# Infini-attention with a GeGLU FFN on one core: two phases, transposed scores, four heads per PE tile set, softmax without maximum behind a guard

## Chip, cores, metric

One core of one Trainium2 chip. The metric is the device time of one execution in microseconds (us), median over several runs; lower is better.

## The reference, cut to what matters

x is 2048 x 448 (bf16), 16 heads of 28, four segments of 512 rows, FFN width 1792. Inside a segment the attention is causal; between segments a linear memory is read and then updated.

```python
xn = layernorm(x)
for s in range(4):                                   # segments of 512 rows
    logits = qs @ ks.T * 28**-0.5 + causal_mask
    a_dot = softmax(logits) @ vs
    pq = phi(qs)                                     # phi(t) = t+1 if t>0 else exp(t)
    a_mem = (pq @ M) / (pq @ z + 1e-6)
    o = g * a_mem + (1 - g) * a_dot                  # g = sigmoid(beta), one per head
    M, z = M + phi(ks).T @ vs, z + phi(ks).sum()
s = concat(o) @ wo
g = silu((gelu(xn @ w_gate) * (xn @ w_up)) @ w_down)
out = x + s * g
```

## The kernel before

Segment by segment: load x, layer norm, projection, attention, memory update, FFN, store. In attention, one step takes one block of 128 queries and two heads. Scores have queries on partitions; DVE masks, takes the maximum and negates it; ACT takes the exponential; the result is transposed on PE, copied back from PSUM by DVE and ACT, and multiplied with V, 29 columns at a time (28 and a column of ones, which yields the denominator).

```python
        def stage_scores(j, hp):
            w = (j + 1) * P
            s_ps = ps_big.tile([P, 2, 512], F32, name="big")
            for i in range(2):
                g, hh = divmod(2 * hp + i, HG)
                nc.tensor.matmul(out=s_ps[:, i, 0:w],
                                 lhsT=qT[hh * HP:(hh + 1) * HP, g, j * P:(j + 1) * P],
                                 rhs=kT[hh * HP:(hh + 1) * HP, g, 0:w], start=True, stop=True)
            nc.vector.tensor_tensor(out=s_ps[:, :, j * P:w], ..., in1=cmask..., op=ALU.add)   # cut
            nc.vector.reduce_max(out=mx[:], in_=s_ps[:, :, 0:w], axis=AX.X)
            nc.vector.tensor_scalar(out=nb_[:], in0=mx[:], scalar1=-scale, scalar2=None, op0=ALU.mult)
            for i in range(2):
                nc.scalar.activation(out=p_sb[:, i, 0:w], in_=s_ps[:, i, 0:w], func=ACT.Exp,
                                     bias=nb_[:, i:i + 1], scale=scale)
            return p_sb

        def stage_pv(j, hp, p_sb, o_v3):
            for i in range(2):
                h = 2 * hp + i
                for kb in range(j + 1):
                    nc.tensor.transpose(pt_ps[:, kb, :], p_sb[:, i, kb * P:(kb + 1) * P], ident[:])
                # cut: copy pt_ps to pt_sb, on DVE for i == 0, on ACT for i == 1
                for kb in range(j + 1):
                    nc.tensor.matmul(out=o_v3[:, h, 0:Dh + 1], lhsT=pt_sb[:, kb, :],
                                     rhs=va[:, kb, h, 0:Dh + 1], start=(kb == 0), stop=(kb == j))
        # cut: per query block, reciprocal of the denominators, memory read, mix, transposes, output projection
        # cut: memory update, then the FFN of the same segment
```

Of the kernel before, what the change touches and what calls it, by code (L numbers as in the profile page):

```python
# [8 lines left out]
ACT = mybir.ActivationFunctionType  # L9
ALU = mybir.AluOpType  # L10
F32 = mybir.dt.float32
BF16 = mybir.dt.bfloat16
AX = mybir.AxisListType


@with_exitstack
def kernel(
    ctx: ExitStack,
    tc: tile.TileContext,
    A_x: bass.AP,  # L20
# [9 lines left out]
    out: bass.AP,  # L30
):
    nc = tc.nc
    P = 128
    x2 = A_x.flatten_outer_dims()
    o2 = out.flatten_outer_dims()
    S, D = x2.shape
    F = B_w_gate.shape[1]
    H = A_beta.shape[0]
    Dh = D // H
    NSEG = 4  # L40
    L = S // NSEG
    NB = L // P
    HP = 32
    HG = 3
    G = (H + HG - 1) // HG
    GP = HG * HP

    def gsz(g):
        return min(HG, H - g * HG)
    DC = 112  # L50
    NDC = D // DC
    NFC = F // P
    scale = float(Dh) ** -0.5
    EPS = 1e-5
    assert D == NDC * DC and H * Dh == D and F == NFC * P and L == NB * P
    assert Dh < HP and NB * P <= 512 and H * HP <= 512

    const = ctx.enter_context(tc.tile_pool(name="const", bufs=1))
    wld = ctx.enter_context(tc.tile_pool(name="wld", bufs=1))
    segp = ctx.enter_context(tc.tile_pool(name="segp", bufs=2))  # L60
    work = ctx.enter_context(tc.tile_pool(name="work", bufs=2))
    seg1 = ctx.enter_context(tc.tile_pool(name="seg1", bufs=1))
    attn = ctx.enter_context(tc.tile_pool(name="attn", bufs=3))
    small = ctx.enter_context(tc.tile_pool(name="small", bufs=4))
# [4 lines left out]
    ident = const.tile([P, P], BF16, name="ident")  # L69
# [2 lines left out]
    make_causal_mask(nc, cmask[:], mask_val=-1e9)  # L72
    bdmask = const.tile([GP, GP], F32, name="bdmask")
    nc.vector.memset(bdmask[:], 0.0)
    for i in range(HG):
        nc.vector.memset(bdmask[i * HP:(i + 1) * HP, i * HP:(i + 1) * HP], 1.0)

    beta_bf = const.tile([P, H], A_beta.dtype, name="beta_bf")
# [5 lines left out]
                            op0=ALU.mult, op1=ALU.add)  # L84
# [11 lines left out]
    wo_sb = const.tile([DC, NDC, D], A_wo.dtype, name="wo_sb")  # L96
    wg_sb = const.tile([DC, NDC, F], B_w_gate.dtype, name="wg_sb")
    wu_sb = const.tile([DC, NDC, F], B_w_up.dtype, name="wu_sb")
    wd_sb = const.tile([P, NFC, D], B_w_down.dtype, name="wd_sb")

    def late_weight_loads():
# [10 lines left out]
                          in_=wq_raw[:].rearrange("p c (h d) -> p c h d", d=Dh))  # L112
    nc.gpsimd.tensor_copy(out=wkp[:, :, :, 0:Dh],
                          in_=wk_raw[:].rearrange("p c (h d) -> p c h d", d=Dh))

    vaug = []
    pkb = []
    for i in range(2):
        v_t = const.tile([P, NB, H, HP], BF16, name=f"vaug{i}")
# [3 lines left out]
        k_t = const.tile([P, NB, H, HP], BF16, name=f"pkb{i}")  # L123
        nc.gpsimd.memset(k_t[:], 0.0)
        pkb.append(k_t)
    macc = const.tile([GP, G, GP], F32, name="macc")
    mbd = const.tile([GP, G, GP], BF16, name="mbd")

# [7 lines left out]
    x_v = x2.rearrange("(s b p) d -> s p b d", p=P, b=NB)  # L136
    o_v = o2.rearrange("(s b p) d -> s p b d", p=P, b=NB)

    for s in range(NSEG):
        use_mem = s > 0  # L140
        upd_mem = s < NSEG - 1
        va = vaug[s % 2]
        pk = pkb[s % 2]
# [7 lines left out]
        for b in range(NB):  # L151
# [5 lines left out]
                                op0=ALU.add)  # L157
# [14 lines left out]
        for g in range(G):  # L172
            n = gsz(g) * HP
            for (wp, dst, is_q) in ((wqp, qT, True), (wkp, kT, False)):
                pr = ps_acc.tile([P, L], F32, name="acc")
                for c in range(NDC):
                    nc.tensor.matmul(  # L177
                        out=pr[:n, :],
                        lhsT=wp[:, c, g * HG:g * HG + gsz(g), :].rearrange("p h d -> p (h d)"),
                        rhs=xnT[:, c, :], start=(c == 0), stop=(c == NDC - 1))  # L180
                nc.scalar.copy(out=dst[:n, g, :], in_=pr[:n, :])  # L181
                if is_q and use_mem:
                    phi(pqT[:n, g, :], pr[:n, :], [P, L], n)
# [22 lines left out]
        def stage_scores(j, hp):  # L206
            w = (j + 1) * P
            s_ps = ps_big.tile([P, 2, 512], F32, name="big")
            for i in range(2):
                g, hh = divmod(2 * hp + i, HG)  # L210
                nc.tensor.matmul(out=s_ps[:, i, 0:w],  # L211
                                 lhsT=qT[hh * HP:(hh + 1) * HP, g, j * P:(j + 1) * P],
                                 rhs=kT[hh * HP:(hh + 1) * HP, g, 0:w],
                                 start=True, stop=True)
            nc.vector.tensor_tensor(out=s_ps[:, :, j * P:w], in0=s_ps[:, :, j * P:w],  # L215
                                    in1=cmask[:].unsqueeze(1).to_broadcast([P, 2, P]),
                                    op=ALU.add)
            mx = small.tile([P, 2], F32, name="mx")
            nc.vector.reduce_max(out=mx[:], in_=s_ps[:, :, 0:w], axis=AX.X)  # L219
            nb_ = small.tile([P, 2], F32, name="nb_")  # L220
            nc.vector.tensor_scalar(out=nb_[:], in0=mx[:], scalar1=-scale, scalar2=None,
                                    op0=ALU.mult)
            p_sb = attn.tile([P, 2, L], BF16, name="p_sb")
# [4 lines that stand above are left out]
# [77 lines left out]
        if upd_mem:  # L305
            for g in range(G):
                n = gsz(g) * HP
                hs = slice(g * HG, g * HG + gsz(g))
                u_ps = ps_acc.tile([P, L], F32, name="acc")
                for b in range(NB):  # L310
                    nc.tensor.matmul(
                        out=u_ps[:n, 0:n],
                        lhsT=pk[:, b, hs, :].rearrange("p h d -> p (h d)"),
                        rhs=va[:, b, hs, :].rearrange("p h d -> p (h d)"),
                        start=(b == 0), stop=(b == NB - 1))
                if s == 0:
                    nc.vector.tensor_tensor(out=macc[:n, g, 0:n], in0=u_ps[:n, 0:n],
                                            in1=bdmask[:n, 0:n], op=ALU.mult)
                else:
                    um = work.tile([GP, GP], F32, name="um")  # L320
                    nc.vector.tensor_tensor(out=um[:n, 0:n], in0=u_ps[:n, 0:n],
                                            in1=bdmask[:n, 0:n], op=ALU.mult)
                    nc.gpsimd.tensor_tensor(out=macc[:n, g, 0:n], in0=macc[:n, g, 0:n],
                                            in1=um[:n, 0:n], op=ALU.add)
                nc.gpsimd.tensor_copy(out=mbd[:n, g, 0:n], in_=macc[:n, g, 0:n])
# [22 lines left out]
        nc.sync.dma_start(out=o_v[s], in_=o_out[:])  # L348


# [1 line left out]
_INS = ['A_x', 'A_wq', 'A_wk', 'A_wv', 'A_wo', 'A_beta', 'B_x', 'B_w_gate', 'B_w_up', 'B_w_down']  # L352
_OUTS = [((1, 2048, 448), 'bfloat16')]
# [25 lines left out]
```

## Time and profile before

| | before |
|---|---|
| median of 4 runs | 570.84 us (566.3 to 573.75) |
| span of the profiled run, mean granted clock of PE | 566.7 us, 0.762 |
| start, until attention | 42 us |
| four attention stages | 296 us |
| three projection stages between segments | 72 us |
| four FFN stages | 150 us |
| end | 7 us |

The prediction below shows the lines and reads them.

### The profile page before, as it was taken

What the parts mean: (1) busy time and instruction counts of PE and PEld (TensorE: products, weight loads), DVE (VectorE), ACT (ScalarE), POOL (GpSimd) and SP (SyncE); (2) the same over time, 40 slices, a digit from 0 to 9 for tenths busy, and PEclk for the clock granted to TensorE, in tenths of its full rate; (3) what the DMA queues carried; (4) which work ended last, traced back from release to release, by engine and by line L of the source; (5) the groups of instructions that cost most, each with busy time, mean ns of one, the idle gap of its engine ahead of it and who ended that gap; (6) DMA issues with size and microseconds to landing.
All of it is one profiled execution on the core that took longest, in us unless ns stands there. A gap on an engine that the chain in (4) does not pass through costs nothing.

```text
span 566.7 us, 7756 instructions
## 1 busy us (share of the span) xinstructions
PE 446.8 (79%) x2864; PEld 226.6 (40%) x2864; DVE 333.0 (59%) x826; ACT 301.6 (53%) x605; POOL 70.2 (12%) x91
## 2 busy tenths in 40 slices
PE   0776877899976679688997677768999867968895
PEld 0432444444532334344453233434445433434342
DVE  7338787643057787765308778784422678776430
ACT  1465666544357566563447655656335656656441
POOL 9000000010600000003060000000214000000006
PEclk9995565599977555579999655576999955557998
DMA  7910000000010000000010000000000000000000
GB/s 189 275 56 1 1 0 2 1 0 2 33 33 0 2 0 2 2 0 2 1 38 29 1 1 0 2 2 0 1 1 32 1 1 2 0 2 1 0 1 33
DMA packets 6422, 10.59 MB, mean 19 GB/s; under 512 B 384, under 2 KB 5392, under 8 KB 6384
## 3 DMA queue, kind: packets, MB, share of 16 engines
q0 software_dynamic: 1088, 5.62, 3.6%
q1 hardware_dynamic: 4368, 3.67, 2.2%
q10 hardware_dynamic: 928, 0.80, 0.5%
q8 instruction: 22, 0.36, 0.3%
q14 instruction: 16, 0.13, 0.1%
HBM read 8.26 MB, written 1.84 MB: 18 GB/s over the span
## 4 chain that ended last, share of the span: by engine, by line
PE 59%; DVE 16%; ACT 13%; DMA 4%; issue 4%; POOL 3%; SPq 0%; POOLq 0%; ACTq 0%; DVEq 0%
PE big L332 17%; PE tp L234 10%; PE acc L342 7%; PE acc L177 7%; ACT p_sb L225 6%; DVE mx L219 5%; PE big L211 5%; PE acc L286 4%; DVE big L215 4%; DMA x_sb<-in_A_x_dram 4%; ACT pt_sb L240 3%; PE big L189 2%; POOL o_sb L272 2%; PE acc L242 2%; DVE pt_sb L238 2%
## 5 line engine op out<-in xcount | busy, mean ns | idle before, releaser
L234 PE MATMUL tp<-ident,p_sb 128*128 128x128 bf16 x640 | 100.2, 283 | 19.0 <-ACT p_sb L225 16.4
L219 DVE TENSOR_REDUCE mx<-big 128x2 f32<-128x256 f32 (+3 forms) x128 | 104.4, 816 | 1.6
L240 ACT COPY pt_sb<-tp 128x128 bf16<-128x128 bf16 (+3 forms) x128 | 54.5, 426 | 57.6 <-PE tp L234 52.8
L211 PE MATMUL big<-kT,qT 32*128 32x128 bf16 (+3 forms) x256 | 61.3, 420 | 15.3 <-ACT p_sb L225 12.7
L215 DVE TENSOR_TENSOR big<-big,cmask 128x256 f32<-128x256 f32 x128 | 55.0, 430 | 27.4 <-PE big L211 14.3
L234 PEld LDWEIGHTS <-p_sb 128*128 128x128 bf16 x640 | 53.4, 119 | 42.1 <-ACT p_sb L225 37.3
L242 PE MATMUL acc<-vaug,pt_sb 128*128 128x29 bf16 x640 | 56.0, 192 | 16.8 <-DVE pt_sb L238 7.4
L336 DVE TENSOR_TENSOR hT<-gl,big 128x512 bf16<-128x512 bf16 x56 | 38.4, 686 | 51.2 <-ACT gl L335 51.2
L335 ACT ACTIVATE gl<-big 128x512 bf16<-128x512 f32 x56 | 33.0, 597 | 57.4 <-PE big L332 57.3
L242 PEld LDWEIGHTS <-pt_sb 128*128 128x128 bf16 x640 | 38.3, 108 | 62.8 <-DVE pt_sb L238 17.9
L332 PE MATMUL big<-xnT,wg_sb 112*128 112x512 bf16 x224 | 62.9, 397 | 0.5 <-DVE hT L336 0.5
L332 PE MATMUL big<-xnT,wu_sb 112*128 112x512 bf16 x224 | 61.5, 387 | 0.0
L238 DVE COPY pt_sb<-tp 128x128 bf16<-128x128 bf16 (+3 forms) x128 | 40.8, 319 | 31.6 <-PE tp L234 28.9
L342 PE MATMUL acc<-wd_sb,hT 128*128 128x448 bf16 x224 | 43.0, 352 | 0.0
L177 PE MATMUL acc<-xnT,wqp 112*96 112x512 bf16 (+1 forms) x96 | 27.2, 409 | 7.9 <-ACT kT L181 7.9
L177 PE MATMUL acc<-xnT,wkp 112*96 112x512 bf16 (+1 forms) x96 | 28.5, 425 | 6.0 <-DVE pqT L133 6.0
L332 PEld LDWEIGHTS <-wg_sb 112*128 112x128 bf16 x224 | 22.2, 101 | 23.8 <-issue 2.0
L189 PE MATMUL big<-wkv,xnT 112*128 112x448 bf16 x128 | 30.2, 362 | 1.9 <-DVE pkb L199 1.7
L211 PEld LDWEIGHTS <-qT 32*128 32x128 bf16 x256 | 16.1, 98 | 37.7 <-issue 30.5
L281 PE MATMUL tp<-ident,o_sb 128*112 128x128 bf16 x64 | 9.8, 301 | 26.8 <-POOL o_sb L272 23.3
L332 PEld LDWEIGHTS <-wu_sb 112*128 112x128 bf16 x224 | 21.7, 99 | 22.8
L342 PEld LDWEIGHTS <-hT 128*128 128x128 bf16 x224 | 21.9, 98 | 20.7
(355 smaller groups left out, 539.7 us busy)
## 6 DMA issues: line engine op xcount, KB each, us to landing
x_sb<-in_A_x_dram SPq DMA_DIRECT2D x4, 448.0 KB, 6.6
out_dram<-o_out SPq DMA_DIRECT2D x4, 448.0 KB, 2.9
wg_sb<-in_B_w_gate_dram POOLq DMA_DIRECT2D x1, 1568.0 KB, 10.2
wu_sb<-in_B_w_up_dram POOLq DMA_DIRECT2D x1, 1568.0 KB, 16.3
wd_sb<-in_B_w_down_dram POOLq DMA_DIRECT2D x1, 1568.0 KB, 19.9
wk_raw<-in_A_wk_dram ACTq DMA_DIRECT2D x1, 392.0 KB, 5.4
wo_sb<-in_A_wo_dram ACTq DMA_DIRECT2D x1, 392.0 KB, 11.3
wq_raw<-in_A_wq_dram POOLq DMA_DIRECT2D x1, 392.0 KB, 9.0
```

The lines of the kernel that those rows point to most:

```text
L177: nc.tensor.matmul(out=pr[:n, :], lhsT=wp[:, c, g * HG:g * HG + gsz(g), :].rearrange("p h d -> p (h d)"), rhs=xnT[:, c, :], start=(c == 0) ...
L189: nc.tensor.matmul(out=kv[:, i, 0:D], lhsT=xnT[:, c, b * P:(b + 1) * P], rhs=wkv[:, c, i * D:(i + 1) * D], start=(c == 0), stop=(c == NDC ...
L211: nc.tensor.matmul(out=s_ps[:, i, 0:w], lhsT=qT[hh * HP:(hh + 1) * HP, g, j * P:(j + 1) * P], rhs=kT[hh * HP:(hh + 1) * HP, g, 0:w], start ...
L215: nc.vector.tensor_tensor(out=s_ps[:, :, j * P:w], in0=s_ps[:, :, j * P:w], in1=cmask[:].unsqueeze(1).to_broadcast([P, 2, P]), op=ALU.add)
L219: nc.vector.reduce_max(out=mx[:], in_=s_ps[:, :, 0:w], axis=AX.X)
L234: nc.tensor.transpose(pt_ps[:, kb, :], p_sb[:, i, kb * P:(kb + 1) * P], ident[:])
L238: nc.vector.tensor_copy(out=pt_sb[:, 0:j + 1, :], in_=pt_ps[:, 0:j + 1, :])
L240: nc.scalar.copy(out=pt_sb[:, 0:j + 1, :], in_=pt_ps[:, 0:j + 1, :])
L242: nc.tensor.matmul(out=o_v3[:, h, 0:Dh + 1], lhsT=pt_sb[:, kb, :], rhs=va[:, kb, h, 0:Dh + 1], start=(kb == 0), stop=(kb == j))
L332: nc.tensor.matmul(out=gu[:, i, :], lhsT=w_sb[:, c, fc * P:(fc + 1) * P], rhs=xnT[:, c, :], start=(c == 0), stop=(c == NDC - 1))
L336: nc.vector.tensor_tensor(out=hT[:, fc, :], in0=gl[:], in1=gu[:, 1, :], op=ALU.mult)
L342: nc.tensor.matmul(out=d_ps[:, 0:D], lhsT=hT[:, fc, b * P:(b + 1) * P], rhs=wd_sb[:, fc, :], start=(fc == 0), stop=(fc == NFC - 1))
```

## The change

The intent: shorten the chain around the exponential. (1) Scores are made transposed, keys on partitions, so the exponential's output is already the operand of the product with V: no transposes and no copies. (2) Four heads share the PE array: scores use row strips of 32, V products use four column strips. (3) The softmax takes no maximum; a guard on the norms of wq and wk bounds the logits, and if it fails, the old kernel runs as a fallback. (4) The causal triangle is set to zero on POOL after the exponential. (5) Denominators go through DRAM, to be inverted compactly and loaded back broadcast over the rows of a head. (6) All attention first, then all FFN, so the output projection of attention is taken in the FFN phase.

```diff
+        BANKS = (((0, 0),), ((1, 0), (3, 384)), ((2, 0),))
+        def scores(s, g, bk):
+            w = sum(L - kb * P for kb, _ in BANKS[bk])
+            for pr in range(2):
+                sp = ps_s.tile([P, 2, L], F32, name="s")
+                for kb, c0 in BANKS[bk]:
+                    n = L - kb * P
+                    for j in range(2):
+                        r = slice((2 * pr + j) * HP, (2 * pr + j + 1) * HP)
+                        nc.tensor.matmul(out=sp[:, j, c0:c0 + n],
+                                         lhsT=kT[s][r, g, kb * P:(kb + 1) * P],
+                                         rhs=qT[s][r, g, kb * P:L], start=True, stop=True)
+                pt = ptp.tile([P, 2, L], BF16, name="pt")
+                nc.scalar.activation(out=pt[:, :, 0:w], in_=sp[:, :, 0:w], func=ACT.Exp, scale=scale)
+                for kb, c0 in BANKS[bk]:
+                    v = pt[:, :, c0:c0 + P]
+                    nc.gpsimd.affine_select(out=v, in_=v, pattern=[[0, 2], [1, P]],
+                                            compare_op=ALU.is_ge, fill=0.0, base=0, channel_multiplier=-1)
+        def pv(s, g, bk, pts, acc):    # cut: n = L - kb * P, va = V and ones of segment s
+            for kb, c0 in BANKS[bk]:
+                for i in range(HG):
+                    nc.tensor.matmul(out=acc[i * HP:(i + 1) * HP, kb * P:L],
+                                     lhsT=va[:, kb, g * HG + i, :], rhs=pts[i // 2][:, i % 2, c0:c0 + n],
+                                     start=(kb == 0), stop=(kb == 2), tile_position=(0, i * HP))
+        def evac(s, g, side, ps):          # side 0: attention, side 1: memory; cut: t, a result tile oU of a pool of 5 per side
+            nc.vector.tensor_copy(out=t[:], in_=ps[:])
+            nc.sync.dma_start(out=den[s][side, g * HG:(g + 1) * HG, :], in_=t[Dh:P:HP, :])
+        def normalise(s):
+            # ... cut: load den as 128 x 64, add 1e-6, times 1/gate, reciprocal, store to rdr
+            for g in range(G):
+                for side in range(ns):
+                    r = rbp.tile([P, L], F32, name=f"rb{side}")
+                    nc.sync.dma_start(out=r[:],
+                        in_=rdr[side, g * HG:(g + 1) * HG, :].unsqueeze(1).to_broadcast([HG, HP, L]))
+                    rb.append(r)
+                # cut: rb = the group's tiles, o_a and o_n its results, the case s == 0 without memory
+                nc.gpsimd.tensor_tensor(out=o_a[:], in0=o_a[:], in1=rb[0][:], op=ALU.mult)
+                nc.gpsimd.tensor_tensor(out=o_n[:], in0=o_n[:], in1=rb[1][:], op=ALU.mult)
+                nc.gpsimd.tensor_tensor(out=dst, in0=o_a[:], in1=o_n[:], op=ALU.add)
...
+        for s in range(NSEG):              # phase 1
+            # ... cut: load x(s+1); per group and bank: scores, the pending V product, evac, memory read;
+            # ... cut: normalise(s) once its last group is out; layer norm and projection of s+1; update(s)
+        ok = nc.values_load(oki[0:1, 0:1], min_val=0, max_val=1)
+        tc.no_sync_barrier()
+        for s in range(NSEG):              # phase 2: FFN as before, plus oT @ wo
...
+    ok = fast_path(tc, ...)
+    with tc.If(ok == 0, preferred_fallthrough_block=False):
+        general_path(tc, ...)              # the kernel before
```

## The prediction

> **What bounds the kernel now.** I read the page's busy shares and its slices first, to see whether one engine is full.
>
> ```profile
> span 566.7 us, 7756 instructions
> PE 446.8 (79%) x2864; PEld 226.6 (40%) x2864; DVE 333.0 (59%) x826; ACT 301.6 (53%) x605; POOL 70.2 (12%) x91
> ...
> PEclk9995565599977555579999655576999955557998
> ```
>
> No engine is full, and the granted clock changes between about 5 and 10 tenths four times: there are stages of two kinds, once per segment. So I cut the span by stage (columns: busy us of PE, weight load, DVE, ACT, POOL, then the granted clock).
>
> ```profile
> 0.00:42.00 42.00, 21.12 (x98) 11.29 (x99) 20.03 (x46) 17.44 (x29) 13.76 (x17) 1.00 0.65 175
> 42.00:113.00 71.00, 54.01 (x404) 28.03 (x403) 53.54 (x142) 43.56 (x99) 0.00 (x0) 0.54 0.00 1
> 113.00:151.00 38.00, 37.38 (x219) 18.65 (x217) 12.86 (x26) 14.52 (x24) 7.91 (x12) 1.00 0.00 1
> 151.00:176.00 25.00, 18.65 (x78) 9.13 (x76) 13.63 (x31) 16.54 (x29) 2.16 (x2) 0.86 0.13 37
> 176.00:253.00 77.00, 58.03 (x433) 29.76 (x433) 58.56 (x158) 46.13 (x104) 3.38 (x3) 0.56 0.00 1
> 560.00:567.00 7.00, 0.00 (x0) 0.00 (x0) 0.00 (x0) 0.31 (x1) 2.16 (x2) 0.72 0.19 66
> ```
>
> The pattern repeats. The four attention stages (42 to 113, 176 to 253, 315 to 395, 453 to 521) last 296 us, the four FFN stages 150, the three projection stages between segments 72, the start 42, the end 7. An FFN stage is PE-bound at full clock: 37.4 of 38 us. An attention stage has PE and DVE both at about 75% and the clock at 0.54 to 0.60: a chain of short hand-offs at a slow clock. The chain of waits and the cost groups say which ones.
>
> ```profile
> PE big L332 17%; PE tp L234 10%; PE acc L342 7%; PE acc L177 7%; ACT p_sb L225 6%; DVE mx L219 5%; PE big L211 5%; PE acc L286 4%; DVE big L215 4%; DMA x_sb<-in_A_x_dram 4%; ACT pt_sb L240 3%; PE big L189 2%; POOL o_sb L272 2%; PE acc L242 2%; DVE pt_sb L238 2%
> ...
> L234 PE MATMUL tp<-ident,p_sb 128*128 128x128 bf16 x640 | 100.2, 283 | 19.0 <-ACT p_sb L225 16.4
> L219 DVE TENSOR_REDUCE mx<-big 128x2 f32<-128x256 f32 (+3 forms) x128 | 104.4, 816 | 1.6
> L240 ACT COPY pt_sb<-tp 128x128 bf16<-128x128 bf16 (+3 forms) x128 | 54.5, 426 | 57.6 <-PE tp L234 52.8
> L215 DVE TENSOR_TENSOR big<-big,cmask 128x256 f32<-128x256 f32 x128 | 55.0, 430 | 27.4 <-PE big L211 14.3
> L242 PE MATMUL acc<-vaug,pt_sb 128*128 128x29 bf16 x640 | 56.0, 192 | 16.8 <-DVE pt_sb L238 7.4
> L238 DVE COPY pt_sb<-tp 128x128 bf16<-128x128 bf16 (+3 forms) x128 | 40.8, 319 | 31.6 <-PE tp L234 28.9
> ```
>
> Around the exponentials there is masking (55.0), maximum (104.4), 640 transposes (100.2), copies of them (54.5 on ACT, 40.8 on DVE) and 640 products only 29 columns wide (56.0). All of this goes or shrinks. Last, the timeline, for the durations I need.
>
> ```profile
> 510.13 0.39 PE L211 MATMUL big<-kT,qT 32*128 32x512 bf16 x1
> 510.88 0.39 PE L211 MATMUL big<-kT,qT 32*128 32x512 bf16 x2
> 513.05 1.27 ACT L225 ACTIVATE p_sb<-big,nb__5581 128x512 bf16<-128x512 f32 x2 [0.58 <-DVE nb__5581 L221]
> ...
> L346 POOL TENSOR_TENSOR sl<-sl,sA 128x448 f32<-128x448 f32 x16 | 18.1, 1131 | 94.6 <-ACT sl L345 94.6
> masks.py:199 POOL TENSOR_SCALAR_AFFINE_SELECT ident<-ident 128x128 bf16<-128x128 bf16 x1 | 0.3, 296 | 0.0
> ```
>
> One score matmul of 512 columns takes 0.39 us, and two of them, in different row strips, also take 0.39 us together, at the full clock of that stretch. One streams for 0.217 (90 FFN matmuls of 512 columns take 19.53 us in the chain), so two in series would take about 0.6: they ran side by side.
>
> **What the Trainium skill says.** "TensorEngine Tiling (Array Packing)", Key Properties: different tiles execute loads and matmuls in parallel, and changing the tiling mode drains the engine. The pair above agrees with the first; no trace here shows the second. Its Performance Considerations add that tiling "speeds up TensorE but not PSUM evacuation", which is why I expect ACT, not PE, as the floor of the softmax itself. "TensorE: Matmul & The Clock Gate", Part 1: the clock is half when the array has not been busy, full after some 3.4 us of sustained work; the trace agrees (0.54 to 0.60 in attention, 1.00 in FFN). "GPSIMD Engine Reference", section 3.1: two-input elementwise work costs about 2.6 cycles per element; the trace's 1131 ns for 448 is 2.5 ns each, rather worse. "DMA: Bandwidth & Descriptors", Anatomy of one DMA: about 2 us fixed; the 448 KB stores of this trace land in 2.9.
>
> **The change, part by part.** All attention now comes first, then all FFN. Scores are made transposed (keys on partitions), so the exponential's output feeds the product with V directly.
>
> *ACT.* Per segment and group of four heads, exponentials of 1024, 1024, 1024, 1024, 512 and 512 columns. The timeline's two of 512 in 1.27 us, each 0.69 long, put the second 0.58 after the first; 384 columns take 0.578 and 512 take 0.690, so 1024 is about 0.58 + 0.45 = 1.03. Sum: 16 x (4 x 1.03 + 2 x 0.58) = 84.5 us, against 120 busy for the same lines before. With 24 exponentials for phi at 0.55 to 0.60: 98 us in the attention phase.
>
> *DVE.* Mask, maximum, negation and copies go (220 us). It takes over the PSUM copies: 32 of Q and K and 28 of results at about 0.69, 16 of V at 0.6, phi 24, layer norm 26, the rest 5: about 106 us.
>
> *POOL.* 128 triangle selects of 256 elements, about 0.40 each (0.296 for 128, plus 128 at memset's 0.84 ns): 51. Normalisation, 40 tensor_tensors of 512 at 1.29 (1131 ns scaled): 52. Updates 6: about 109 us, where before it had 14 in the attention stages.
>
> *PE, at full clock.* Scores come in pairs, since two heads share a PSUM tile and the other two wait for the second: 2 x 1280 columns per group, 1.07 us, x16 = 17. The product with V has four column strips together: 1280 columns, 0.53 us, x16 = 8.5. Projection: 128 of 512 at 0.217 and 112 of 448 at 0.19 = 49 (six groups of three heads become four of four, so 64 fewer). Transposes 6.5, updates 3.4, memory reads 2.6. Sum 87 us; at the attention clock of 0.56 it is 155.
>
> *DMA.* The denominators go to DRAM and back: store, load, reciprocal, store, broadcast loads, four round trips of about 2 us per segment. It frees DVE of per-row work, but DVE and POOL are in-order, so a late landing holds the triangle selects behind it.
>
> *FFN.* The same 448 matmuls at 0.217 (97.2), 224 at 0.1895 (42.4: 56 took 10.61) and 64 output projections (12.1): 152 us, already at full clock before. No gain.
>
> **Attention phase in sum.** ACT 98, DVE 106, POOL 109, PE 87 to 155: four engines balanced, so none hides behind another. Projections and layer norm of the next segment have PSUM of their own and depend only on x; instructions are not issued strictly in program order (in the trace FFN matmuls begin at 109.5 while attention products run at 113), so I let them overlap attention. With POOL at the 75% that the old attention reached on its busiest engines: 109 / 0.75 = 145; with PE at a clock of 0.65, 87 / 0.65 = 134 plus drains and waits of some 20. Four segments at about 36 plus three normalisation hand-offs at about 4: I choose 158 us. The start falls to about 36 (x lands at 13 as now, layer norm 8, projection 13 to 15). Entering FFN: 5 for the last round trip, which stands before FFN's multiplies on DVE. End 7, branch over the fallback path 4 (my guess). Sum: 36 + 158 + 5 + 152 + 11 = 362; measured time is 4 over the span now, so **366 us**, 36% less.
>
> **The rivals.**
> 1. *POOL and DMA serialise the segments.* If normalisation stands in POOL's queue ahead of the next segment's selects, each segment boundary costs some 9 us of round trips plus 12 multiplies and adds (15), less about 5 of work ahead: 20 x 3, giving about 415. For: strict order within an engine, POOL at 1131 ns for 448. Against: the order seen is chosen by readiness.
> 2. *PE at half clock is the bound.* 87 us become 174 with drains on top: attention 190, total about 400. For: clock 0.50 in most attention windows although PE is marked 75% busy. Against: a PE that becomes the bound is dense and gets its clock back, as the old projections did (0.86 to 1.00).
> 3. *Everything overlaps.* Attention 115 to 120, total about 325. For: balanced engines, separate PSUM. Against: the old attention with two stages in flight never passed 77%.
> 4. *The guard and fallback cost more than a branch.* Waiting for the guard value or skipping 7000 instructions: +5 to +20. Nothing in this trace shows it.
>
> **Range and chances.** Rivals 1 and 2 span 400 to 415, rival 3 gives 325; together they make 328 to 415. For no gain at all attention would have to cost 350 us, more than before; only a mistake in kind would do that. Faster by over 2%: 0.98; within 2%: 0.01; slower: 0.01.
>
> **What would show it.** Right: a first phase of about 195 us with exponentials on ACT near 85 us, POOL over 100 us busy, and a second phase of about 155 to 160 us at clock 1.00 with PE full. Score pairs of 512 columns in one streaming time, V products four to a streaming time. Rival 1: POOL idle for DMA with selects late, ACT idle about 20 us at each boundary. Rival 2: attention windows at 0.50 with PE full. Wrong outright: matmuls in column strips running in series (PE 25 us longer at full clock), selects of far over 0.4 us, or an FFN clock below 1.

## The result and the profile after

376.92 us median of 4 runs (376.23 to 378.08), against 570.84. The ratio is 0.6609, with a 95% interval of 0.6572 to 0.6646. A ratio here is the mean time of one kernel's fast runs over that of the other's fast runs of the same rounds, so not quite the ratio of the medians. The output is correct; the fallback was not taken.

The page of the changed kernel, its span, busy times and granted clock:

```profile
span 375.8 us, 4396 instructions
PE 308.9 (82%) x1619; PEld 128.8 (34%) x1620; DVE 159.6 (42%) x297; ACT 146.4 (39%) x203; POOL 142.0 (38%) x207
PEclk9999999995559965559855589999999999999998
```

DVE and ACT have half the work that they had (333.0 and 301.6 us), POOL twice (70.2). The clock row splits in two: from the middle on full clock, in the first part three dips to half. Cut by stage (columns: busy us of PE, weight load, DVE, ACT, POOL, then clock, DMA share, GB/s):

```profile
0.00:37.30 37.30, 15.25 (x52) 6.06 (x53) 23.02 (x51) 1.58 (x3) 16.38 (x15) 1.00 0.79 209
37.30:214.70 177.40, 140.02 (x834) 50.25 (x833) 86.65 (x173) 93.64 (x121) 94.02 (x164) 0.74 0.10 36
214.70:368.40 153.70, 153.66 (x736) 72.48 (x736) 49.27 (x74) 51.14 (x80) 30.61 (x27) 0.99 0.12 36
```

The attention phase, with the projections of three segments inside it, takes 177.4 us, where attention and projections took 296 + 72 = 368. That is 190.6 of the 190.9 us by which the span fell; the start gave about 5 and the FFN took back about 4. The costliest groups of the new attention phase (in each line: busy us, mean ns of one, then the idle time of the engine before them and what ended most of it):

```profile
L252 ACT ACTIVATE pt<-s 128x1024 bf16<-128x1024 f32 (+1 forms) x96 | 81.8, 881 | 93.4 <-PE s L248 66.7
L255 POOL TENSOR_SCALAR_AFFINE_SELECT pt<-pt 128x256 bf16<-128x256 bf16 x128 | 52.9, 432 | 64.2 <-ACT pt L252 63.4
L266 PE MATMUL pv<-pt,vaug 128*32 128x128 bf16 (+3 forms) x256 | 37.7, 378 | 21.6 <-POOL pt L255 21.1
L248 PE MATMUL s<-qT,kT 32*128 32x128 bf16 (+3 forms) x256 | 43.0, 361 | 7.2 <-POOL mbd L234 5.0
L312 POOL TENSOR_TENSOR oU<-oU,rb 128x512 f32<-128x512 f32 x12 | 15.2, 1266 | 20.9 <-DVE hT L362 12.4
```

The exponentials (81.8) stand alone where maximum, mask, transposes and copies stood around them. But ACT waits 66.7 us for scores, and PE waits 21.1 us for the selects that POOL makes. Where those waits lie is seen in stretches of 10 us:

```profile
100.00:110.00 10.00, 10.00 (x50) 2.40 (x51) 2.79 (x7) 6.14 (x8) 3.32 (x8) 0.50 0.00 1
130.00:140.00 10.00, 2.59 (x25) 1.04 (x22) 1.13 (x2) 4.38 (x6) 7.74 (x9) 0.69 0.26 102
140.00:150.00 10.00, 5.13 (x27) 1.86 (x26) 3.94 (x6) 2.05 (x2) 8.29 (x9) 0.50 0.25 91
```

At the boundary of two segments (130 to 150) PE works 7.7 of 20 us, POOL 16.0, and the DMA share stands at a quarter. Between boundaries (100 to 110) PE is marked busy all the time, but at half clock. The timeline of the boundary, with lines on strips first and last (start, duration; in brackets the idle time before and what ended it):

```profile
130.49 0.40 PE L266 MATMUL pv<-pt,vaug 128*32 128x512 bf16 x4
136.70 1.26 POOL L233 TENSOR_TENSOR macc<-macc,um 128x512 f32<-128x512 f32 x1
139.12 0.61 POOL L234 CAST mbd<-macc 128x512 bf16<-128x512 f32 x1
139.79 1.03 PE L282 MATMUL m<-pqT,mbd 128*128 128x512 bf16 x2 [4.92 <-POOL mbd L234]
145.15 1.02 ACT L252 ACTIVATE pt<-s 128x1024 bf16<-128x1024 f32 x1 [9.11 <-PE pv L266]
...
207.12 0.60 PE L248 MATMUL s<-qT,kT 32*128 32x512 bf16 x1
208.74 0.61 PE L248 MATMUL s<-qT,kT 32*128 32x512 bf16 x2
```

PE waits 4.92 us for the memory's bf16 copy, which stands in POOL's queue between normalisation multiplies, and at 145.15 ACT has been idle for 9.11 us, until V products let it go on. The last two lines, both at half clock: one score matmul of 512 columns takes 0.60 us, two in different row strips take 0.61. They run side by side. So do column strips: in the first line, at full clock, four V products of 512 columns take 0.40 us, and in series they would take 0.87 (an estimate: four times the 0.217 of the prediction's FFN matmuls).

Why is the DMA share a quarter? The broadcast loads have a slowest dimension of 4 (the heads of a group). The Trainium skill, "DMA: Bandwidth & Descriptors", section "Why a DMA increments its semaphore by 16 and not by 1", says that a load uses the largest number of engines up to 16 that divides the slowest dimension of both sides: 4. The trace agrees: share 0.26 at 102 GB/s, so one load of 256 KB takes about 2.6 us, and eight of them about 21 us at a boundary (an estimate; the first boundary has four loads, as segment 0 reads no memory).

### The profile page after: what moved, and what is told of

Its sections match the earlier page's. It is cut to its first block, busy times and chain, and to the rows that moved or that the text cites. A ratio compares the mean times of both kernels' runs of the same rounds, so it can differ in the third digit from the quotient of the medians.

```text
span 375.8 us, 4396 instructions
## 1 busy us (share of the span) xinstructions
PE 308.9 (82%) x1619; PEld 128.8 (34%) x1620; DVE 159.6 (42%) x297; ACT 146.4 (39%) x203; POOL 142.0 (38%) x207
## 5 line engine op out<-in xcount | busy, mean ns | idle before, releaser
L252 ACT ACTIVATE pt<-s 128x1024 bf16<-128x1024 f32 (+1 forms) x96 | 81.8, 881 | 93.4 <-PE s L248 66.7
L255 POOL TENSOR_SCALAR_AFFINE_SELECT pt<-pt 128x256 bf16<-128x256 bf16 x128 | 52.9, 432 | 64.2 <-ACT pt L252 63.4
L362 DVE TENSOR_TENSOR hT<-gl,s 128x512 bf16<-128x512 bf16 x56 | 38.2, 687 | 63.5 <-ACT gl L361 63.5
L358 PE MATMUL s<-xnT,wg_sb 112*128 112x512 bf16 x224 | 58.8, 386 | 0.1
L358 PE MATMUL s<-xnT,wu_sb 112*128 112x512 bf16 x224 | 58.4, 384 | 0.0
L361 ACT ACTIVATE gl<-s 128x512 bf16<-128x512 f32 x56 | 33.1, 597 | 63.5 <-PE s L358 63.5
L266 PE MATMUL pv<-pt,vaug 128*32 128x128 bf16 (+3 forms) x256 | 37.7, 378 | 21.6 <-POOL pt L255 21.1
L248 PE MATMUL s<-qT,kT 32*128 32x128 bf16 (+3 forms) x256 | 43.0, 361 | 7.2 <-POOL mbd L234 5.0
L367 PE MATMUL pv<-wd_sb,hT 128*128 128x448 bf16 x224 | 44.3, 352 | 0.0
L182 PE MATMUL m<-xnT,wq_pad 112*128 112x512 bf16 x64 | 22.3, 468 | 6.9 <-DVE qT L186 5.5
L312 POOL TENSOR_TENSOR oU<-oU,rb 128x512 f32<-128x512 f32 x12 | 15.2, 1266 | 20.9 <-DVE hT L362 12.4
L374 ACT ACTIVATE sl<-pv 128x448 f32<-128x448 f32 x16 | 8.7, 544 | 26.8 <-PE pv L367 26.8
```

The costliest lines, as they stand in the source:

```text
L182: nc.tensor.matmul(out=pr[:], lhsT=wpad[nm][:, c, g * HG:(g + 1) * HG, :].rearrange("p h d -> p (h d)"), rhs=xnT[:, c, s, :], start=(c == ...
L248: nc.tensor.matmul(out=sp[:, j, c0:c0 + n], lhsT=kT[s][r, g, kb * P:(kb + 1) * P], rhs=qT[s][r, g, kb * P:L], start=True, stop=True)
L252: nc.scalar.activation(out=pt[:, :, 0:w], in_=sp[:, :, 0:w], func=ACT.Exp, scale=scale)
L255: nc.gpsimd.affine_select(out=v, in_=v, pattern=[[0, 2], [1, P]], compare_op=ALU.is_ge, fill=0.0, base=0, channel_multiplier=-1)
L266: nc.tensor.matmul(out=acc[i * HP:(i + 1) * HP, kb * P:L], lhsT=va[:, kb, g * HG + i, :], rhs=pts[i // 2][:, i % 2, c0:c0 + n], start=(kb ...
L312: nc.gpsimd.tensor_tensor(out=o_a[:], in0=o_a[:], in1=rb[0][:], op=ALU.mult)
```

## The experiments

Two things hold for all of them. First, the build arranges each engine's stream anew for each kernel, so an edit also moves the order of instructions that it does not touch; where that matters, it is said. Second, each was timed in three rounds beside the kernel before (571 us); all profiled runs were fast unless said.

**1. The normalisation's 40 multiplies and adds on DVE instead of POOL**

```diff
-  nc.gpsimd.tensor_tensor(out=o_a[:], in0=o_a[:], in1=rb[0][:], op=ALU.mult)   # and the three like it
+  nc.vector.tensor_tensor(out=o_a[:], in0=o_a[:], in1=rb[0][:], op=ALU.mult)
```

> The changed kernel with the normalisation's 40 multiplies and adds moved from POOL to DVE; nothing else. Theory 1 (POOL's queue: the attention phase, 178 us against the 158 predicted, loses its time at segment boundaries because triangle selects stand behind normalisation arithmetic in one in-order queue): the ACT gaps of 9 us at 136 to 145 us and after 190 us shrink, total 352 to 364 us. Theory 2 (the DRAM round trip: what holds the queue is the landing of the broadcast loads, whoever waits): the same wait moves to DVE, which also copies projections and results out of PSUM, total 370 to 385 us.

Measured: 398.31 us, ratio 0.6995 (0.6953 to 0.7036); 21 us slower than the changed kernel, and outside the ranges of both theories. Attention does end earlier, with the last V product at 204.8 and not 214.2. But the timeline at the entry to the FFN shows the loss:

```profile
217.32 0.69 DVE L312 TENSOR_TENSOR oU<-oU,rb 128x512 f32<-128x512 f32 x1 [6.82 <-DMA rb<-rdr]
219.99 0.69 DVE L313 TENSOR_TENSOR oU<-oU,rb 128x512 f32<-128x512 f32 x1 [1.98 <-DMA rb<-rdr]
...
238.90 1.86 PE L358 MATMUL s<-xnT,wg_sb 112*128 112x512 bf16 x4 [26.56 <-DVE hT L362]
```

DVE waits for each load of the last segment, one every 2.6 us or so, and the FFN's own multiply stands behind them in DVE's queue: PE is idle for 26.56 us. So in this build the loads are slow, and a slow load costs what stands behind it in the same queue. On POOL, the last segment's normalisation lies beside the FFN, and PE does not wait there.

**2. x of the second segment loaded before the FFN weights**

```diff
+        load_x(1)
         nc.sync.dma_start(out=wg_sb[:], ...)
...
-            if s + 1 < NSEG:
+            if 1 < s + 1 < NSEG:
```

> The changed kernel with the load of the second x segment issued ahead of the three FFN weight loads. In the trace DVE stands idle 7.2 us at 22 to 29 us before the layer norm statistics of segment 1, whose x lands behind 4.7 MB of weights, and PE waits 5.5 us for DVE's copy behind it. If that is the start's loss: total 5 to 7 us less, 370 to 372 us. Rival: the start is bound by the POOL squares and layer norm in any case or the time is given back at the first boundary: total within 2 us of 377.

Measured: 378.09 us, ratio 0.6632 (0.6592 to 0.6673); no gain. The first exponential starts at 28.4 and not 37.3, yet the last V product starts at 215.2 against 214.2. The nine microseconds are all given back in the phase, as the rival had it. What takes them back was not looked for.

**3. Normalisation with a constant in place of the loads (wrong)**

```diff
-                    r = rbp.tile([P, L], F32, name=f"rb{side}")
-                    nc.sync.dma_start(out=r[:], in_=rdr[side, ...].to_broadcast([HG, HP, L]))
-                    rb.append(r)
+                rb = [rb_c] * ns            # one tile of ones
```

> Wrong results on purpose: the normalisation multiplies by a constant tile, so its arithmetic stays on POOL but nothing waits for the 28 broadcast loads, which are gone. Theory 1 (POOL's arithmetic in the queue): the boundaries stay, only the 20 us of POOL waits for those loads go and part of them is hidden; total 364 to 374 us. Theory 2 (the round trip holds the queue): the boundary gaps close, total 340 to 358 us.

Measured: 365.11 us median, two runs fast (359.95 and 362.39), two slow; the ratio of the fast runs is 0.6338 (0.6285 to 0.6392), which is 4.1% less than the changed kernel's 0.6609, some 15 us. That lies between the two expected ranges, so neither theory alone. The edit takes away all waiting for the denominators (store, inversion, loads), not the loads only, and keeps the multiplies: about 15 us, from two runs, is the price of the whole round trip. The profiled run was one of the slow ones.

**4. The memory update's add and copy on DVE instead of POOL**

```diff
-                nc.gpsimd.tensor_tensor(out=macc[:], in0=macc[:], in1=um[:], op=ALU.add)
-            nc.gpsimd.tensor_copy(out=mbd[:], in_=macc[:])
+                nc.vector.tensor_tensor(out=macc[:], in0=macc[:], in1=um[:], op=ALU.add)
+            nc.vector.tensor_copy(out=mbd[:], in_=macc[:])
```

> The changed kernel with only the memory update's add and bf16 copy (5 instructions) moved from POOL to DVE. PE waits for that copy 4.9 + 10.7 us in the trace, with scores and V products queued behind. If the copy's place in POOL's queue is what opens the 9 us gap at the boundary: total 8 to 14 us less, 363 to 369 us. If the selects behind normalisation would hold PE there anyway: within 3 us of 377.

Measured: 374.59 us, ratio 0.6589 (0.6543 to 0.6635): 2 us, within the intervals of both. The rival came true; more was expected. The wait for that copy was real (4.92 us), but PE's wait for selects grew: by the groups, V products wait 31.7 us for POOL's selects, where it was 21.1. The selects stand in the same queue as the multiplies. Taking one victim out of a queue leaves the others in it; that this is why the gain did not come is argued.

**5. Each broadcast load split by head**

```diff
-                    nc.sync.dma_start(out=r[:],
-                        in_=rdr[side, g * HG:(g + 1) * HG, :].unsqueeze(1).to_broadcast([HG, HP, L]))
+                    for i in range(HG):
+                        nc.sync.dma_start(out=r[i * HP:(i + 1) * HP, :],
+                            in_=rdr[side, g * HG + i:g * HG + i + 1, :].to_broadcast([HP, L]))
```

> The changed kernel with each 256 KB broadcast load of reciprocals split into four loads, one per head (32 partitions each); same bytes. Theory 3: what misses in the attention phase is the landing of these loads, because one whose slowest dimension is 4 runs on 4 of the 16 DMA engines: during them the trace shows a DMA share of 0.26 at 101 GB/s, and they land 2.6 us apart. If so the share rises well above 0.5 in those stretches, and the total falls most of the way to the run without these loads (365): 362 to 370 us. Rival: reading one row into 32 partitions is slow at the memory's side: share rises but the spacing stays near 2.6 us, total 374 to 380.

Measured: 365.26 us, ratio 0.6411 (0.6382 to 0.6439): 12 us less, in the expected range. The expected sign, a DMA share well above 0.5, did not come: it is 0.36 from 120 to 130 us and 0.23 from 130 to 140. The last V product starts at 192.0 and not 214.2, so the attention phase is 22 us shorter, but not all of it arrives. The two lines are from the queue that issues the loads and from PE at the entry to the FFN:

```profile
119.38 24.54 SPq L303 DMA_DIRECT2D rb<-rdr  x32
206.09 1.87 PE L359 MATMUL s<-xnT,wg_sb 112*128 112x512 bf16 x4 [5.24 <-DVE hT L363]
```

The 32 small loads occupy the issuing queue for 24.54 us: 13.4 us of issuing (an estimate, 32 at the median of 0.42), the rest waiting, for free tiles among other things. Stores of denominators wait behind them, the last normalisation starts late, and PE stands before the FFN for 5.24 us. The gain is less clean than it looks: in this build POOL takes up to five selects between two multiplies, in the changed kernel mostly one. So faster loads and another order came together, and this run does not divide the 22 us between them.

**6. The kernel before without maximum and negation**

```diff
-            nc.vector.reduce_max(out=mx[:], in_=s_ps[:, :, 0:w], axis=AX.X)
-            nc.vector.tensor_scalar(out=nb_[:], in0=mx[:], scalar1=-scale, ...)
...
-                                     bias=nb_[:, i:i + 1], scale=scale)
+                                     scale=scale)
```

> The kernel before with one part of the change alone: no maximum and no negation (exponential without bias), all else kept, transposes too. It takes 104 + 20 us from DVE. If DVE held the old attention stages: 296 us of them fall to 250 to 270, total 515 to 545 us. Rival: the chain through scores, mask, exponential, transpose, copy, product at half PE clock holds it and DVE's work was beside it: total 550 to 572 us.

Measured: 492.04 us, ratio 0.8628 (0.8581 to 0.8674): 79 us less, more than expected, and correct on these inputs. DVE falls from 333.0 to 229.6 us busy, and the mean clock rises from 0.762 to 0.813. Three quarters of the DVE time removed (103.4) came off the end: the maximum was on the chain between score and exponential, as the prediction read it.

**7. The kernel before in two phases**

```diff
-        xnT = segp.tile([DC, NDC, L], BF16, name="xnT")      # sA likewise
+        xnT = keep.tile([DC, NDC, L], BF16, name="xnT")      # four kept
...
+        kept[s] = (xnT, sA)
+    tc.no_sync_barrier()
+    for s in range(NSEG):                                    # x loaded again
         hT = seg1.tile([P, NFC, L], BF16, name="hT")
```

> The kernel before with the other part alone: all attention first, then all FFN (projection input and attention output of the four segments kept in SBUF, x loaded again), the attention itself unchanged. Theory: order alone gives little, since each FFN stage already ran at full clock with PE full: total within 2% of 570. Rival: the gain of the change is largely that next segment's projection may run under attention once FFN is out of the way: 72 us of projection stages mostly hidden, total 510 to 540 us.

Measured: 582.79 us, ratio 1.0223 (1.0178 to 1.0269): 2.2% more, just outside the expected 2%, and with this interval it is not clear that the loss passes 2%. The edit also keeps sA (attention's result) in bf16. The order alone gives nothing. A likely reason, argued and not shown, is that the FFN's dense matmuls no longer fill the ragged ends of attention (they began at 109.5, before attention ended at 113, in the kernel before).

**8. Strips taken away, instruction count kept (wrong)**

```diff
-                        r = slice((2 * pr + j) * HP, (2 * pr + j + 1) * HP)
+                        r = slice(0, HP)                     # every score in row strip 0
...
-                    nc.tensor.matmul(out=acc[i * HP:(i + 1) * HP, kb * P:L], lhsT=va[:, kb, g * HG + i, :], ...
-                                     tile_position=(0, i * HP))
+                    nc.tensor.matmul(out=acc[:, kb * P:L], lhsT=va[:, kb, g * HG:(g + 1) * HG, :]...)   # full width
```

> Wrong results on purpose: the changed kernel with the same number of matmuls and columns, but all score matmuls in row strip 0 and each V product over the full array, so that none can run beside another. If the strips are what makes scores and V products cheap, PE gets 17 + 25 us more at full clock and up to twice that at half: total 405 to 450 us. Rival: the attention phase is held by ACT and POOL and PE has slack: total below 390 us.

Measured: 419.75 us, ratio 0.7369 (0.7331 to 0.7406): 43 us more, as expected. The result check called the output correct, although every head here uses the scores of its group's head 0: on these inputs the check says little about the details of attention, here and elsewhere. The groups of this kernel:

```profile
L266 PE MATMUL pv<-pt,vaug 128*128 128x512 bf16 (+3 forms) x256 | 67.6, 396 | 16.5 <-POOL pt L255 16.4
L248 PE MATMUL s<-qT,kT 32*128 32x512 bf16 (+3 forms) x256 | 65.7, 379 | 0.1
```

The duration of one matmul hardly moves (396 against 378 ns, 379 against 361), but the time in which PE is occupied by them goes from 37.7 to 67.6 and from 43.0 to 65.7 us: 52.6 us together, of which 43 reach the end. That is the price of the strips in this pair of builds; how much of it a moved order of instructions makes up was not separated.

**9. One load per head and side, for all four groups**

The tile holds all groups (128 x 4 x 512); to make room, the squares of the guard share one buffer, the scratch tile um of the memory update loses its second copy, and the reciprocals have one buffer each.

```diff
-            for g in range(G):
-                for side in range(ns):
-                    r = rbp.tile([P, L], F32, name=f"rb{side}")
-                    nc.sync.dma_start(out=r[:], in_=rdr[side, ...].to_broadcast([HG, HP, L]))
+            for side in range(ns):
+                r = rbp.tile([P, G, L], F32, name=f"rb{side}")
+                for i in range(HG):
+                    nc.sync.dma_start(out=r[i * HP:(i + 1) * HP, :, :],
+                        in_=rdr[side].rearrange("(g i) l -> i g l", i=HG)[i:i + 1].to_broadcast([HP, G, L]))
```

> The changed kernel with the reciprocals broadcast in one load per head and side for all four groups (28 loads of 256 KB, each with slowest dimension 32) into single tiles; the squares share a buffer and one scratch tile loses its second copy, to make room. With loads per head and group (365.3) the sync queue's 112 issues of 0.42 us held the denominator stores behind them for up to 24 us, and FFN then began with a 10 us gap on PE. If that queue is what is left: 352 to 360 us, FFN's entry gap under 5 us. Rival: the entry gap is the round trip itself: 362 to 367.

Measured: 372.53 us, ratio 0.6539 (0.6512 to 0.6566): only 4 us less, 7 more than experiment 5, and outside both its ranges, a miss. The loads are now quick, as the stretch of the second boundary shows, and still (the last line is DVE's copy of a memory read out of PSUM):

```profile
120.00:130.00 10.00, 8.15 (x69) 3.49 (x67) 5.13 (x10) 6.38 (x9) 4.79 (x10) 0.97 0.84 191
...
140.00:150.00 10.00, 0.44 (x4) 0.20 (x2) 0.00 (x0) 1.60 (x3) 10.00 (x13) 0.50 0.00 0
...
L273 DVE COPY oU<-m 128x512 f32<-128x512 f32 x12 | 8.2, 691 | 54.3 <-POOL oT L313 48.4
```

DMA share 0.84 at 191 GB/s, all landed by about 133. Then, from 140 to 150, POOL is busy for 10.00 of 10 us, mostly with multiplies and adds, no DMA runs, PE works 0.44 us and ACT 1.60. What waits is seen at its end: DVE's copy at 150.46 has waited 21.20 us for POOL's add, and PE's memory read at 151.20 has waited 10.25 us for that copy. The copy writes a result tile, of which there are five per side, and a tile is free only when POOL has normalised what stands in it. So POOL's slow work holds buffers: these copies wait 48.4 us in all for POOL's add, where it was 13.2 in the changed kernel. The selects, which might be suspected, stand here before the multiplies (five of them at 144.91), and PE's wait for them in front of V products is 5.7 us (21.1 in the changed kernel). The order of POOL's work moved along with the loads, so that the loads' gain was lost to this wait is argued; no run has more result tiles, which would test it.

**10. Experiment 9 with 2 and 4 added**

The edits are those shown there.

> The same, plus the memory update's add and copy on DVE and x of segment 1 loaded before the FFN weights. Alone these two gave -2 and +1 us, the second because nine microseconds won at the start were waited off at the first hand-off. If the hand-off is cured, both count: 6 to 12 us less than the loads alone. Rival: within 3 us of it.

Measured: 364.02 us, ratio 0.6384 (0.6357 to 0.6410): 8.5 us less than experiment 9, as expected. POOL is still full from 140 to 150, and DVE's copies still wait for POOL's add (46.1 us in all). With quick loads, the two edits that gave nothing alone (0 and 2 us) together give more. That each had been hidden behind another wait fits, but is not shown.

**11. Experiment 10 with the normalisation of segments 0 to 2 on DVE, of the last on POOL**

```diff
-  nc.gpsimd.tensor_tensor(out=o_a[:], in0=o_a[:], in1=rb[0], op=ALU.mult)      # and the three like it
+  (nc.vector if s < NSEG - 1 else nc.gpsimd).tensor_tensor(out=o_a[:], in0=o_a[:], in1=rb[0], op=ALU.mult)
```

> The same as the run before, plus the normalisation's multiplies and adds on DVE for all segments but the last (which stays on POOL, so that DVE is free for FFN's entry). Moved whole onto DVE with slow loads it took 9 us off the attention phase and lost 30 at FFN's entry. With fast loads, if POOL's queue still holds selects behind arithmetic: 5 to 12 us less than the run before. Rival: with the loads fast POOL keeps up, within 3 us of it, or slower by DVE's waits.

Measured: 337.57 us (336.14 to 337.92), ratio 0.5914 (0.5886 to 0.5941): 26.5 us less than experiment 10, far more than the expected 5 to 12, correct, and faster than both kernels (0.895 of the changed one, by the two ratios). Span 336.0, clock 0.934. Attention runs from 33.6 to 174.9, 141 us against 177.4, and the FFN follows without a gap. The stretch of its second boundary, which here lies at 120 to 130, then three groups:

```profile
120.00:130.00 10.00, 8.23 (x48) 2.43 (x49) 9.75 (x14) 6.67 (x10) 7.33 (x12) 0.55 0.01 3
...
L274 DVE COPY oU<-m 128x512 f32<-128x512 f32 x12 | 8.1, 686 | 6.4 <-PE m L280 4.2 <-PE s L246 2.2
L253 POOL TENSOR_SCALAR_AFFINE_SELECT pt<-pt 128x256 bf16<-128x256 bf16 x128 | 61.9, 504 | 87.5 <-ACT pt L250 86.0
L314 DVE TENSOR_TENSOR oT<-oU,oU 128x512 bf16<-128x512 f32 x8 | 6.8, 884 | 0.0
```

DVE now does the multiplies (9.75 of 10 us busy), and PE works 8.23 of 10 us, where it worked 2.92 from 140 to 150 in experiment 10. DVE's copies no longer wait for POOL's add at all (46.1 us in experiment 10). PE's wait for selects in front of V products falls to 4.5 us by the groups (8.2 in experiment 10, 21.1 in the changed kernel). The move is not free: a select takes 504 ns on the mean (432 in the changed kernel), and the DVE add 884 (719 in experiment 1). The Trainium skill, "GPSIMD Engine Reference", section 1, says that POOL shares its SBUF interfaces with DVE and contends with DVE instructions that have two SBUF inputs; the trace agrees in kind, by these numbers. So with quick loads the multiplies are better on DVE at three boundaries. That the last belongs on POOL, where DVE is needed for the FFN, rests on experiment 1 with its slow loads; all of it on DVE with quick loads was not run.

**12. No guard, no branch, no fallback**

```diff
-        sqs = {}                             # squares, norms, oki: 22 lines
...
-        ok = nc.values_load(oki[0:1, 0:1], min_val=0, max_val=1)
...
-    with tc.If(ok == 0, preferred_fallthrough_block=False):
-        general_path(tc, ...)
```

> The changed kernel without the weight-norm guard, the branch and the fallback path. The prediction put the branch at 4 us and a rival at up to 20. In the trace the span ends with 2.3 us of issue before the last add and the guard's squares take POOL 6.7 us at the start, before layer norm. Expected 1 to 5 us less, 372 to 376 us. Rival: 8 us or more less (code size, instruction fetch).

Measured: 384.28 us, ratio 0.6731 (0.6700 to 0.6762): 7 us *more*, a miss in sign. The first exponential starts at 26.8 (37.3), but the last V product at 224.3 (214.2). The same stretch in the changed kernel, then in this one:

```profile
60.00:70.00 10.00, 9.96 (x63) 3.46 (x63) 6.08 (x14) 8.21 (x11) 5.45 (x11) 1.00 0.01 4
```

```profile
50.00:60.00 10.00, 9.12 (x48) 2.47 (x46) 5.45 (x14) 6.13 (x9) 3.87 (x10) 0.62 0.17 47
60.00:70.00 10.00, 10.00 (x41) 2.26 (x40) 3.04 (x6) 5.37 (x7) 4.46 (x9) 0.50 0.01 3
```

Without the guard the phase falls to half clock already at 50 us: PE is marked busy all of the time from 60 to 70, but the trace has 41 matmuls there where the changed kernel has 63. The compiled streams of PE, DVE, ACT and POOL stand in another order too; on POOL, for one, the layer norms of later segments stand between other selects. Whether the order, the earlier start or the clock's own history is the cause, this run does not tell. It does show that leaving out guard and branch in this way gains nothing.

## Why the prediction was right, and where its sum was off

The direction and the mechanism held, and 376.92 lies in the range of 328 to 415. By the terms of its sum, against the profiled run (377.6 us):

| term | predicted | measured | difference |
|---|---|---|---|
| start to first exponential | 36 | 37.3 | +1.3 |
| attention phase | 158 | 177.4 | +19.4 |
| entering FFN | 5 | 0 | -5 |
| FFN | 152 | 153.7 | +1.7 |
| end and branch | 11 | 7.4 | -3.6 |
| time over span | 4 | 1.8 | -2.2 |
| sum | 366 | 377.6 | +11.6 |

- *Durations.* Exponentials 84.5 predicted, 81.8 measured (one of 1024 columns 1.018 us at the median). Selects 0.40 each, 0.408 at the median and 0.432 on the mean. POOL multiplies 1.29, measured 1.266. POOL's work of attention: 109 predicted; 94.0 in the phase and 15 of the last normalisation beside the FFN. These were right.
- *Strips.* Predicted as pairs in one streaming time; the 0.60 and 0.61 us show it, and experiment 8 prices it at 43 us. The overlap was right, the size less so: scores and V products were put at 25.5 us at full clock and are marked busy for 80.7 (43.0 and 37.7), part of it at half clock and with waits inside the marks. PE as a whole is marked busy for 140 us in the phase, inside the predicted 87 to 155.
- *DVE and ACT.* Predicted 106 and 98 us in the phase, measured 86.7 and 93.6.
- *FFN.* "No gain" was right: 153.7 us, PE full at 0.99.
- *What brought the gain.* Experiment 6 shows that removing the maximum is worth 79 us in the old structure, experiment 7 that the two phases alone are worth nothing. The rest of the 191 us (transposes, their copies, short V products, masking) was not taken apart, but for the 43 us of the strips in experiment 8; that it comes from there is argued from the rows that vanished.
- *The term that was mis-sized.* "Three normalisation hand-offs at about 4" us, from "four round trips of about 2 us". PE's idle time shows what they are: it is 37.4 us in the phase, of which 33 lie in the stretches around the boundaries (5.1 from 80 to 100, 13.8 from 130 to 160, 14.4 from 180 to 210), so about 11 each. The latencies were about right: the DMA that depends on another is issued 1.7 us after it (117.60 and 119.28) or 1.5 (124.41 and 125.92). What the sum left out is the bytes on 4 of 16 engines (some 21 us of broadcast loads at a boundary) and POOL's multiplies in front of others' work. Experiment 3 puts the whole round trip at some 15 us; experiment 11 against 10 puts the multiplies on POOL at 26.5 us once the loads are quick.
- *Its readings of the skill.* The clock in attention (0.54 to 0.60) was called an agreement with the skill's clock page, but PE is marked busy for 76% of those stages, so the agreement is not shown. The figure of about 2 us fixed is given by the page for DMAs that POOL (GpSimd) issues; these are issued by SyncE. And POOL's "rather worse" came from dividing one size: from 448 to 512 elements the time grows from 1131 to 1266 ns, 2.1 ns per element, which is 2.5 cycles at the page's clock of 1.2 GHz and agrees with its 2.6; some 186 ns per instruction are fixed (an estimate from these two sizes, in two kernels).
- *Entering FFN.* The prediction put normalisation ahead of DVE's multiplies; it is on POOL, beside the FFN, so nothing was lost. Experiment 1 shows what its version costs: 26.56 us of idle PE.
- *Rivals.* The first (POOL and DMA serialise the segments) happened in part: ACT idle for 9.11 us at one boundary, against about 20 in the prediction's sign for it. The second (half clock) happened in part too: 0.50 from 100 to 110 us with PE marked full, so "a PE that becomes the bound is dense and gets its clock back" failed there, as far as busy marks can tell. The third did not happen. The fourth has no support: without the guard the kernel was slower.

What stays open: why the clock stays at half for 20 us while PE is marked busy, and with it why experiment 12 is slower. The changed kernel's trace shows a pattern, not a cause: the clock is high where matmuls of the projections, which do not use strips, run (7.7 us of them from 110 to 120 at clock 0.83, 7.5 from 170 to 180 at 1.00), and half where none run (140 to 160, 190 to 210); but 50 to 60 held 1.00 with only 2.6 us of them. No run tests it. Open too: whether more result tiles would have saved experiment 9, and how the 22 us of experiment 5 divide between load speed and order.

## What to carry to other kernels

Shorten the chain around the bottleneck operation before making any engine faster: a layout in which one operation's output is the next one's operand removes the transposes, the copies and their hand-offs at once. Where a slow transfer feeds an engine with an in-order queue, ask what stands behind it there, and place that work on the engine that has nothing urgent behind it at that moment; the right engine can differ between the first and the last segment. Slow work also holds the buffers that it reads: in experiment 9 that cost more waiting (48.4 us) than the instructions behind it in the queue. When an edit gains nothing although its wait was in the trace, look for the next wait behind it and try taking both away together.

## What the Trainium skill lacked or had wrong

- "TensorE: Matmul & The Clock Gate": it gives some 3.4 us of sustained work for full clock. Here PE was marked busy for 10.00 of 10 us at clock 0.50 (100 to 110 us), and for 10.00 of 10 at 0.50 in experiment 12. This is no contradiction, since the page also describes short idle times between groups of matmuls that make the clock fall, and a busy mark need not show them; but it does not say how matmuls in strips count, or how to tell from a trace.
- "GPSIMD Engine Reference": no figure for the affine select; measured 0.408 us for 256 elements per partition at the median and 0.296 for 128. Its 2.6 cycles per element for two-input work agree with the slope measured here (2.5), but the fixed part of some 186 ns per instruction has no figure of its own there. The contention with DVE that it names has sizes here that stand on no page: 432 to 504 ns for a select, 719 to 884 for the DVE add.
- "DMA: Bandwidth & Descriptors": its rule for the number of engines was borne out (share 0.26 and 0.84). It advises joining small transfers; what it does not bring out is that splitting holds up the queue: 32 loads of 64 KB held the issuing queue for 24.54 us (0.42 us each to issue at the median, the rest waits), with small stores behind them.
